# Another order for the products, sums and parts of a Winograd-type matmul kernel

## The chip, the cores and the metric

The kernel runs on one core of one Trainium2 chip. The time is that of one execution on the device in microseconds, the median of several runs. The core's engines are named as in the profile: PE (matmuls), DVE, ACT and POOL (elementwise work), SP (issues nearly all DMAs). Each engine works off its own instructions in the order in which the program issues them and waits on semaphores for the others.

## The reference

Windowed attention (8 batches, 8 heads, 576 positions, head size 64, window 64) makes x with 512 channels per position; an MLP over positions and an MLP over channels follow.

```python
def _moe_ref(x, w_tok1, w_tok2, w_ch1, w_ch2):
    xt = x.transpose(0, 2, 1)
    h = np.maximum(xt @ w_tok1, 0.0) @ w_tok2      # 576 -> 256 -> 576
    u = x + h.transpose(0, 2, 1)
    h2 = np.maximum(u @ w_ch1, 0.0) @ w_ch2        # 512 -> 1536 -> 512
    return (u + h2).astype(np.float32)
```

All values are float32. The change touches the second half, h2 and the sum with u, for 8 x 576 = 4608 positions.

## The kernel before

**Parts.** Every operand of a product is split into a high part (`hi`, a cast to fp32r on ACT) and a low part (`lo`, the source less the high part, a subtraction on DVE or POOL), and each product of two 128-wide operands is three matmuls: hi x hi, hi x lo, lo x hi. A matmul has 512 columns.

**First half** (to about 260 us of the span): attention and the MLP over positions. It stores u in DRAM by chunks of 512 positions (`u_dram`). Nine chunks, 0 to 8, are left for the MLP over channels.

**Plain chunks 0, 1, 2** (260 to 477 us). For each, `gemm1` makes 12 blocks of 128 hidden channels (slots `ft` 0 to 11, 12 matmuls each), followed by `relu_split`: ACT writes ghi, DVE glo. `gemm2` multiplies these with the second weights for four column blocks `ct`; `add_out` adds the result to u on DVE and stores it. Chunk 0 does all 12 slots and then the four blocks; chunks 1 and 2 do it in two halves of six slots (18 matmuls a block). `load_u` and `split_u` fetch and split the next chunk's u (four parts, `uhi` on ACT, `ulo` on DVE). Beside this run generators that the loops push on with `next`:

- `late_steps`: conversion of the second weights in chunk 0 (seven steps per block)
- `weight_steps` (`steps`): sums of the first weights for the pairs, in tiles of the pool `pw`, stored in `w1s`; 16 steps
- `weight_steps2` (`steps2`): the same for the second weights. Six sets, each of five steps: blocks of 512 KB are loaded from DRAM into `w2t`, summed on DVE, cast on ACT into `w2p` and subtracted on DVE; eight stores of 128 KB go to `w2s`. `w2t` and `w2p` lie where the first pair's operands of m7 and m5 are to lie (tags c4, c5), and `w2p` holds one set.
- `quarter_steps2` (`steps3`): stores of weights that are used without a sum, 12 of 384 KB, in chunk 2.

In chunk 2 the first pair's operands are made as well: `load_raw` loads four blocks of u, `sums` and `sum4` form sums on DVE, `prep` splits an operand into `comb`.

**Pairs** (3,4), (5,6), (7,8), 477 to 888 us. Two chunks at a time, the product with each weight matrix uses seven block products instead of eight, `PRODUCTS` = m1, m6, m7, m5, m2, m4, m3. `INTO` gives the PSUM bank of each: m1 and m2 share bank 0, m7 and m4 bank 2, m5 and m3 bank 3, and the later product of the two adds to the bank after the earlier one has been read. A pair has three groups (`grp`), each of two slots `pair_f` (f even with `fi` 0, f odd with `fi` 1; 42 matmuls each) and an output stage `pair_op` (84 matmuls). `pair_f` combines the products on ACT and DVE in x1, x2, x3, applies the ReLU (`block`: r22, r11, r21, r12) and splits. `combine` forms the sums t1, t2, r12, t1 and their parts; for the even slot it is pushed on during the odd one, for the odd slot it runs in the output stage. In the output stage, for t = 0 and 1, the products are added to `common` (m1, m6) or to `ufs` (all others) on DVE; in the last group of a pair `common` is added to `ufs` as well and the result is stored. There (`more`, unless the pair is the last) the next pair's operands are made too: `prep(q + 1, m, 0)` for half of them in the odd slot and the start of the stage, `prep(q + 1, m, 1)` during t = 1. All loads and stores are issued from SP, in program order.

## Time and profile before

| | us |
|---|---|
| median of 3 runs | 891.22 (889.02 to 892.72) |
| the profiled execution | 892.58 |
| its span | 890.6 |
| mean granted clock | 0.971 |
| PE busy | 830.0 (93%) |
| DVE busy | 630.7 (71%) |
| ACT busy | 422.7 (47%) |
| POOL busy | 191.1 (21%) |

A row of groups reads: line, engine, operation, what it writes <- what it reads, shapes, count | busy time, mean ns | idle time of the engine just before and what ended it. A row of waits reads: who waited <- for whom, total us, times, longest us. A row of the timeline: start, duration, instruction, and in brackets the idle time before it with what ended it. A row of windows: the stretch, its length, busy time and count of PE, weight loads, DVE, ACT and POOL, granted clock, share of the DMA engines, GB/s. PE's rows overlap, since matmuls are pipelined.

### The profile page before, as it was taken

The numbers are of one execution on the slowest core, as the hardware profiler recorded it, in microseconds if no ns is written. First come the engines' busy times: TensorE is split into PE (matmuls) and PEld (weight loads), VectorE is DVE, ScalarE is ACT, GpSimd is POOL, SyncE is SP. The second block draws the span as 40 slices with busy tenths as digits, with TensorE's granted clock in tenths as the row PEclk, the third lists the DMA queues.
The fourth block names the chain that finished last, engine by engine and source line by source line (L and its number), as shares of the span: only waits on it lengthen the run. The fifth ranks groups of instructions, "written<-read, shape, count | busy, mean of one in ns | idle before, by whom it ended". The sixth has DMA issues, their size and how long they took to land.

```text
span 890.6 us, 15820 instructions
## 1 busy us (share of the span) xinstructions
PE 830.0 (93%) x5752; PEld 666.2 (75%) x5752; DVE 630.7 (71%) x1545; ACT 422.7 (47%) x1173; POOL 191.1 (21%) x181
## 2 busy tenths in 40 slices
PE   8989999999999899989899999968999986999997
PEld 6668888888898688857688686746777764777775
DVE  5978888898828946774454858676667678675767
ACT  6978988898834303232132423342515152424251
POOL 3623444343310000000001111125202023311021
PEclk9999999999999999989899999997999989999999
DMA  9837877875456477669919482626945444845412
GB/s 351 274 105 253 268 233 242 280 266 196 141 176 214 124 240 209 203 204 290 334 42 381 180 294 100 232 90 220 338 176 204 166 166 151 323 175 194 168 53 94
DMA packets 91357, 185.90 MB, mean 209 GB/s; under 512 B 8848, under 2 KB 56336, under 8 KB 89360
## 3 DMA queue, kind: packets, MB, share of 16 engines
q1 hardware_dynamic: 89168, 183.07, 60.1%
q10 hardware_dynamic: 2112, 1.84, 0.6%
q8 instruction: 45, 0.74, 0.3%
q14 instruction: 32, 0.26, 0.1%
HBM read 140.84 MB, written 44.04 MB: 208 GB/s over the span
## 4 chain that ended last, share of the span: by engine, by line
PE 21%; DVE 16%; ACT 13%; issue 4%; DMA 4%; SPq 1%; ACTq 0%; DVEq 0%
PE op L1041 11%; PE gp L1005 5%; ACT w2hi_r L991 5%; ACT ghic L955 4%; DVE w2lo_r L964 3%; DVE w1lo L959 3%; PE op L665 3%; ACT w1hi L955 2%; PE gp L656 2%; DMA out<-uf 2%; DVE x L1015 1%; DVE w2lo_r L977 1%; DVE m L129 1%; DMA w2t<-w_dram 1%; DVE w2lo_r L967 1%
## 5 line engine op out<-in xcount | busy, mean ns | idle before, releaser
L1005 PE MATMUL gp<-m,w1hi 128*128 128x512 f32 x504 | 158.3, 396 | 7.8 <-DVE x L1013 5.3
L1005 PEld LDWEIGHTS gp<-m,w1hi 128*128 128x128 f32 x504 | 94.4, 190 | 32.6 <-DVE x L1013 9.2
L329 ACT ACTIVATE e<-e,nm 128x128 f32<-128x128 f32 x288 | 112.2, 397 | 5.9 <-DVE nm L321 5.8
L959 POOL TENSOR_TENSOR gloc<-w2hi_r,ghic 128x512 fp32r<-128x512 f32 x18 | 23.2, 1292 | 411.7 <-ACT ghic L955 404.3
L1005 PE MATMUL gp<-m,w1lo 128*128 128x512 f32 x252 | 98.9, 392 | 0.0
L1045 DVE TENSOR_TENSOR uf<-op,uf 128x512 f32<-128x512 f32 (+1 forms) x91 | 61.6, 683 | 28.4 <-PE op L1041 26.3
L1041 PE MATMUL op<-ghic,w2hi 128*128 128x512 f32 (+1 forms) x145 | 60.2, 415 | 15.4 <-DVE uf L1045 7.9
L321 DVE CUSTOM_DVE_ANT_0 e<-s,mask 128x128 f32<-128x128 f32 x288 | 65.3, 285 | 12.1 <-PE s L306 12.0
L991 ACT ACTIVATE w2hi_r<-x 128x512 f32<-128x512 f32 x54 | 34.1, 631 | 65.2 <-DVE x L1015 47.1
L1041 PE MATMUL op<-gloc,w2hi 128*128 128x512 f32 (+1 forms) x145 | 58.7, 405 | 0.0
L1041 PE MATMUL op<-ghic,w2lo 128*128 128x512 f32 (+1 forms) x145 | 58.7, 405 | 0.0
L665 PE MATMUL op<-ghi,w2hi 128*128 128x512 f32 x128 | 53.0, 414 | 5.3 <-ACT ghi L643 5.3
L656 PE MATMUL gp<-uhi,w1hi 128*128 128x512 f32 x144 | 56.1, 390 | 0.1
L656 PE MATMUL gp<-ulo,w1hi 128*128 128x512 f32 x144 | 56.0, 389 | 0.0
L656 PE MATMUL gp<-uhi,w1lo 128*128 128x512 f32 x144 | 56.0, 389 | 0.0
L329 ACT ACTIVATION_READ_ACCUMULATOR e<-e,nm 128x1 f32 x288 | 56.0, 194 | 0.0
L1005 PEld LDWEIGHTS gp<-m,w1lo 128*128 128x128 f32 x252 | 47.8, 190 | 10.3
L665 PE MATMUL op<-glo,w2hi 128*128 128x512 f32 x128 | 53.1, 414 | 2.5 <-DVE glo L644 2.5
L665 PE MATMUL op<-ghi,w2lo 128*128 128x512 f32 x128 | 52.1, 407 | 0.0
L1041 PE MATMUL op<-w1lo,w2hi 128*128 128x512 f32 (+1 forms) x91 | 38.8, 426 | 14.0 <-DVE w1lo L959 14.0
L129 POOL TENSOR_TENSOR xlo<-x,xhi 128x512 fp32r<-128x512 f32 x32 | 41.6, 1300 | 45.3 <-ACT xhi L126 44.6
L1009 ACT COPY x<-gp 128x512 f32<-128x512 f32 x18 | 10.5, 583 | 84.1 <-PE gp L1005 84.1
(166 smaller groups left out, 2029.3 us busy)
## 6 DMA issues: line engine op xcount, KB each, us to landing
v<-vh SPq DMA_DIRECT2D x36, 512.0 KB, 4.2
w1hi<-w1s SPq DMA_DIRECT2D x18, 896.0 KB, 4.8
w1lo<-w1s SPq DMA_DIRECT2D x18, 896.0 KB, 6.5
w2hi<-w2s SPq DMA_DIRECT2D x18, 896.0 KB, 4.7
w2lo<-w2s SPq DMA_DIRECT2D x18, 896.0 KB, 6.5
raw<-wc SPq DMA_DIRECT2D x32, 384.0 KB, 4.7
q<-qh SPq DMA_DIRECT2D x36, 256.0 KB, 4.5
k<-kh SPq DMA_DIRECT2D x7, 1280.0 KB, 8.2
```

The lines of the kernel that those rows point to most:

```text
L129: eng_lo.tensor_sub(lo, src, hi.bitcast(F32))
L321: nc.vector.tensor_tensor_reduce(out=e[:, h], in0=s[:, h], in1=mk, scale=-scale, scalar=MAX_F32, op0=ALU.add, op1=ALU.min, accum_out=nm[:, ...
L329: nc.scalar.activation(e[:, h], e[:, h], AF.Exp, bias=nm[:, g:g + 1], scale=-1.0, accum_out=sm[:, g:g + 1])
L656: nc.tensor.matmul(gp, w[:, w1_at(ft, ct)], x[:, ct], start=(k == 0), stop=(k == 3 * NCT - 1))
L665: nc.tensor.matmul(op, w[:, at], x[:, cols], start=(first and k == 0), stop=(last and k == 3 * len(gs) - 1), skip_group_check=not (first a ...
L955: nc.scalar.copy(ops_g[fi][m][0], made[MADE[m]])
L959: eng.tensor_sub(lo, made[MADE[m]], hi.bitcast(F32))
L964: sub(r["t1"], r["r12"], r["r11"])
L991: nc.scalar.activation(made[name], src, AF.Relu)
L1005: nc.tensor.matmul(b, w[:, at], c[:, h, t], start=(n < 4 and k == 0), stop=(k == 5), skip_group_check=True)
L1041: nc.tensor.matmul(bank[t][INTO[m]][:, cols], w[:, at], ops_g[fi][m][h][:, cols], start=(n < 4 and fi == 0 and j == 0), stop=(j == 2), ski ...
L1045: eng.tensor_add(ufs[c][:, ct, cols], x, ufs[c][:, ct, cols])
```

## The change

No matmul and no operand is added or left out; the order in the queues of PE, ACT, DVE, POOL and SP changes.

- Chunk 0: the split of chunk 1's u goes from slot 8 to the four column blocks. Chunk 1: the split of chunk 2's u goes from slot 8 to slots 10 and 11.
- `steps` go from one to two per column block in the first half of chunk 1. `steps2` go from chunk 1 alone (from the first half's blocks on) to slots 10 and 11 and the second half's blocks of chunk 1 (18 steps) and the first half of chunk 2 (two per slot, the rest at the first block).
- The first pair's operands for t = 0 (m1, m6, m7, m5, m2) go from slots 1 and 2 of chunk 2 to the column blocks after slot 5, those for t = 1 two slots later.
- `prep` can make the high or the low part alone. `combine` makes m5's low part earlier.
- `pair_f`: m1's low part waits in `later` until m4's addition is issued; m2's low part of the odd slot is made in the output stage on DVE instead of POOL. At a pair's first slot (from the second pair on) the t = 0 halves of m1, m6, m7, m5 come first.
- `pair_op`: m1's products with the odd slot come after m6's with the even one; both m2 products come before the t loop instead of between m5 and m4. Next-pair parts have other places and engines; in all but the last pair `common` is added on POOL at the end of the stage.

```diff
@@ -700,9 +700,8 @@
                 split_w2()
             if ft == 3:
                 ul[1] = load_u(1, pu)
-            if ft == 8:
-                split_u(ul[1])
         for ct in range(NCT):
+            split_u(ul[1], (ct,))
             for _ in range(7):
                 next(late, None)
             assert all(n in finished for n in range(len(jobs) - 16, len(jobs) - 12 + 4 * ct))
@@ -858,12 +857,15 @@
 
         SOURCE = {"m1": "r11", "m6": "t2", "m7": "r12", "m5": "t1", "m2": "r21", "m4": "r11", "m3": "r22"}
 
-        def prep(q, m, t, eng=None):
+        def prep(q, m, t, eng=None, part=None):
             if (q, m) not in comb:
                 pool = pb if HOME[m] == "c6" else pu
                 comb[q, m] = pool.tile([P, 2, 2, CHUNK], F32R, name=f"{m}_{q}", tag=HOME[m], bufs=1)
-            c = comb[q, m]
-            split(nc.scalar, eng or nc.vector, c[:, 0, t], c[:, 1, t], raws[SOURCE[m]])
+            c, x = comb[q, m], raws[SOURCE[m]]
+            if part != "lo":
+                nc.scalar.copy(c[:, 0, t], x)
+            if part != "hi":
+                (eng or nc.vector).tensor_sub(c[:, 1, t], x, c[:, 0, t].bitcast(F32))
 
 
         steps, steps2, steps3 = weight_steps(), weight_steps2(), quarter_steps2()
@@ -880,31 +882,23 @@
                     gemm1(j, ft, u, g[-1])
...
-                        if half == 1 and ft % 2:
+                        if ft == 3:
+                            ul[j + 1] = load_u(j + 1, pu)
+                        if ft >= NFT - 2:
+                            split_u(ul[j + 1], (2 * (ft - NFT) + 4, 2 * (ft - NFT) + 5))
                             next(steps2, None)
-                    if last and half == 0:
+                    elif half == 0:
                         next(steps3, None)
...
+                        for _ in range(2):
+                            next(steps2, None)
+                    else:
                         if ft == 6:
                             load_w1(0)
+                        if ft == 8:
                             sums()
-                        if ft in (7, 8):
-                            for m in (("m1", "m6"), ("m7", "m5", "m2"))[ft - 7]:
-                                prep(0, m, 1)
-                        if ft == 9:
+                        for m in {8: ("m1", "m6"), 9: ("m7", "m5"), 10: ("m2",)}.get(ft, ()):
+                            prep(0, m, 1)
+                        if ft == 11:
                             sum4()
...
+                    if j == 1 and half == 0:
+                        for _ in range(1 if ct == NCT - 1 else 2):
+                            next(steps, None)
+                    elif j == 1:
+                        for _ in range(4):
                             next(steps2, None)
...
+                    elif half == 0:
+                        if ct == 0:
+                            for _ in steps2:
+                                pass
+                            sums()
+                        for m in (("m1", "m6"), ("m2",), ("m7",), ("m5",))[ct]:
                             prep(0, m, 0)
+                        if ct == NCT - 1:
+                            load_raw(0, 1)
+                    else:
+                        if ct in (0, 1):
+                            load_w2s(ct)
+                        if ct == 1:
+                            sums(False)
+                            sum4()
+                            for m in ("m4", "m3"):
+                                prep(0, m, 0)
...
             parts_hi(fi, "m6")
+            parts_lo(fi, "m5", nc.vector)
             yield
...
-            parts_lo(fi, "m5", nc.vector)
-            yield
...
             parts_lo(fi, "m7", nc.vector)
             yield
+            yield
             parts_lo(fi, "m4", nc.vector)
-            x1 = x1s[fi]
+            x1, later = x1s[fi], []
...
-                    parts_lo(fi, m, eng)
-
+                    if eng is nc.vector:
+                        later.append(m)
+                    elif eng is not None:
+                        parts_lo(fi, m, eng)
+
+            def product(m, ts, first):
+                n, b, c = PRODUCTS.index(m), bank[INTO[m]], comb[q, m]
+                for k, t in enumerate(ts):
+                    at = slice(o + (n * 2 + t) * P, o + (n * 2 + t + 1) * P)
+                    for j, (w, h) in enumerate(((w1hi, 0), (w1hi, 1), (w1lo, 0))):
+                        nc.tensor.matmul(b, w[:, at], c[:, h, t], start=(first and n < 4 and k == j == 0),
+                                         stop=(k == len(ts) - 1 and j == 2), skip_group_check=True)
...
+            more = q + 1 < len(pairs)
+            begin = q > 0 and f == 0
             next(rest, None)
+            if begin:
+
+                for m in PRODUCTS[:4]:
+                    product(m, (0,), True)
...
+                b = bank[INTO[m]]
+                if begin and n < 4:
+                    product(m, (1,), False)
+                else:
+
+                    product(m, (1, 0) if q == 0 and m in ("m4", "m3") else (0, 1), True)
...
-                    block("r21", x2, "m2", nc.gpsimd)
+                    while later:
+                        parts_lo(fi, later.pop(), nc.vector)
+
+                    block("r21", x2, "m2", None if fi else nc.gpsimd)
...
-                if q + 1 < len(pairs):
-                    if f == NH - 2 and m == "m1":
-                        sums()
-                    if f == NH - 1 and n < 4:
-                        prep(q + 1, m, 0, nc.gpsimd if n % 2 else nc.vector)
+                if more and f == NH - 2 and m == "m1":
+                    sums()
+                if more and f == NH - 1 and n < 5:
+                    prep(q + 1, m, 0, part="hi")
+                    if n < 2:
+                        prep(q + 1, m, 0, nc.gpsimd, part="lo")
...
-            def product(t, m, fi, cols=slice(0, CHUNK)):
+            def product(t, m, fis=(0, 1), first=False, cols=slice(0, CHUNK)):
...
+                for fi in fis:
+                    at = slice(t * SLOT + (n * 2 + fi) * P, t * SLOT + (n * 2 + fi + 1) * P)
+                    for j, (w, h) in enumerate(((w2hf, 0), (w2hf, 1), (w2lf, 0))):
+                        nc.tensor.matmul(bank[t][INTO[m]][:, cols], w[:, at], ops_g[fi][m][h][:, cols],
+                                         start=(n < 4 and fi == j == 0), stop=(fi == fis[-1] and j == 2),
+                                         skip_group_check=True)
...
+            WHERE = {"m7": (1, 2), "m5": (1, 2), "m4": (0, 2), "m3": (1, 0)}
+
+            def evict(t, m):
+                b = bank[t][INTO[m]]
+                if m == "m1" and grp == 0:
+                    nc.scalar.copy(common[t], b)
+                elif m in ("m1", "m6"):
+                    nc.vector.tensor_add(common[t], b, common[t])
+                elif m == "m2":
+                    add(0, t, b)
+                    if last:
+                        store(0, t)
+                else:
+                    c, ct = WHERE[m]
+                    add(c, ct + t, b)
+
+            def add_common(t, m, eng):
+                c, ct = WHERE[m]
+                add(c, ct + t, common[t], eng)
+                store(c, ct + t)
+
...
             for t in range(2):
-                for fi in range(2):
-                    product(t, "m1", fi)
-            for m in PRODUCTS[1:4]:
+                product(t, "m1", (0,))
+            for t in range(2):
+                product(t, "m6", (0,))
+            for t in range(2):
+                product(t, "m1", (1,))
+            for m in ("m7", "m5"):
                 for t in range(2):
-                    product(t, m, 0)
-            for _ in combine(1):
+                    product(t, m, (0,))
+            ops = combine(1)
+            if more:
+
+                prep(q + 1, "m7", 0, part="lo")
+                prep(q + 1, "m5", 0, part="lo")
+                prep(q + 1, "m2", 0, nc.gpsimd, part="lo")
+            for n in range(3):
+                next(ops)
+            parts_lo(1, "m2", nc.vector)
+            evict(0, "m1")
+            product(0, "m2")
+            next(ops)
+            evict(1, "m1")
+            if not (final and last):
+                product(1, "m2")
+            next(ops)
+            if more:
+                sum4()
+                prep(q + 1, "m4", 0, part="hi")
+                prep(q + 1, "m3", 0, part="hi")
+                prep(q + 1, "m3", 0, nc.gpsimd, part="lo")
+            next(ops)
+            evict(0, "m2")
+            if not (final and last):
+                evict(1, "m2")
+            for _ in ops:
                 pass
             if more:
-                for m in PRODUCTS[4:]:
-                    if m == "m4":
-                        sum4()
-                    prep(q + 1, m, 0, nc.gpsimd if m == "m4" else nc.vector)
+                prep(q + 1, "m4", 0, part="lo")
                 load_raw(q + 1, 1)
...
             for t in range(2):
                 end = final and last and t == 1
...
+                for m in ("m6", "m7", "m5", "m4", "m3"):
+                    product(t, m, (1,) if m in PRODUCTS[:4] else (0, 1))
+                    evict(t, m)
+                    if end and m in ("m5", "m4", "m3"):
+                        add_common(t, m, nc.vector)
+                    if more and t == 0 and m == "m3":
                         sums()
-                    if more and t == 1:
-                        if m == "m4":
-                            sum4()
-                        prep(q + 1, m, 1, nc.gpsimd if m in ("m7", "m2", "m3") else nc.vector)
+                        for x in PRODUCTS[:4]:
+                            prep(q + 1, x, 1, part="hi")
+                        prep(q + 1, "m1", 1, nc.gpsimd, part="lo")
+                    if more and t == 1 and m == "m6":
+                        prep(q + 1, "m6", 1, part="lo")
+                        prep(q + 1, "m7", 1, nc.gpsimd, part="lo")
+                        prep(q + 1, "m2", 1, part="hi")
+                        prep(q + 1, "m3", 1, part="hi")
+                    if more and t == 1 and m == "m7":
+                        prep(q + 1, "m5", 1, part="lo")
+                        sum4()
+                        prep(q + 1, "m4", 1, part="hi")
+                    if more and t == 1 and m == "m4":
+                        prep(q + 1, "m2", 1, nc.gpsimd, part="lo")
+                        prep(q + 1, "m4", 1, part="lo")
+                if end:
+
+                    for part in range(LAST_PARTS):
+                        cols = slice(part * CHUNK // LAST_PARTS, (part + 1) * CHUNK // LAST_PARTS)
+                        product(t, "m2", cols=cols)
+                        add(0, t, bank[t][0][:, cols], cols=cols)
+                        store(0, t, cols)
+                elif last and final:
+                    for m in ("m5", "m4", "m3"):
+                        add_common(t, m, nc.gpsimd)
                 load_w2s((q * NGRP + grp + 1) * 2 + t)
+            if more:
+                prep(q + 1, "m3", 1, part="lo")
+                for t in range(2):
+                    for m in ("m5", "m4", "m3"):
+                        add_common(t, m, nc.gpsimd)
```

65 lines of the change are left out of this document (removed).

## The prediction

> **What bounds the kernel now.** Read first: the page, for how full TensorE is and when its clock drops.
>
> ```profile
> span 890.6 us, 15820 instructions
> ...
> PE   830.0 (93%) x5752; PEld 666.2 (75%) x5752; DVE 630.7 (71%) x1545; ACT 422.7 (47%) x1173; POOL 191.1 (21%) x181
> ...
> PEclk9999999999999999989899999997999989999999
> ```
>
> TensorE (PE) is the bound; the profiled execution took 892.6 us, 2.0 around its span, 1.4 over the median of 891.2. The change leaves the matmuls as they are, so only PE's pauses can move. Second, the stages by windows, beside the pace in the chain of waits: 24 matmuls in 5.45 us, 0.227 each.
>
> ```profile
> 518.70 5.45 PE gp L1005 x24
> ...
> 260.10:292.60 32.50, 32.50 (x145) 26.95 (x144) 21.78 (x46) 11.76 (x25) 0.00 (x0) 1.00 0.58 182
> 292.60:330.60 38.00, 34.98 (x145) 27.96 (x144) 25.89 (x57) 9.72 (x21) 0.00 (x0) 0.96 0.63 189
> 330.60:394.80 64.20, 59.89 (x249) 47.91 (x248) 46.55 (x94) 21.12 (x43) 0.00 (x0) 0.95 0.68 202
> ...
> 411.10:434.70 23.60, 20.07 (x73) 14.63 (x72) 12.63 (x24) 7.36 (x15) 0.00 (x0) 0.86 0.94 308
> ...
> 518.60:560.40 41.80, 40.00 (x170) 30.98 (x169) 29.00 (x42) 14.24 (x24) 5.30 (x4) 1.00 0.57 201
> 560.40:619.20 58.80, 45.80 (x170) 34.68 (x169) 41.56 (x58) 21.85 (x38) 19.16 (x14) 0.89 0.49 170
> ...
> 702.80:759.50 56.70, 45.84 (x170) 34.68 (x169) 42.01 (x57) 20.93 (x37) 18.25 (x14) 0.88 0.50 173
> ...
> 843.00:890.60 47.60, 40.63 (x175) 31.11 (x173) 31.87 (x47) 14.23 (x24) 9.17 (x7) 0.99 0.23 83
> ```
>
> After the window come its length, then PE's busy time and rows, and the granted clock third from the end. The first row is undisturbed: 145 rows in 32.5 us. Losses: chunk 0's second product 5.5 us (38.0 less 32.5); chunk 1 7.7 (64.2 less 249 x 0.227); chunk 2 7.0 (23.6 less 73 x 0.227). The other windows are cut at one point of successive groups of a pair, 168 matmuls or 38.1 us each (rows over an edge count twice): an inner group loses 3.6 (six such), the two groups that end a pair 20.7 and 18.6, the last some 6 beside its tail. That is 87 us.
>
> Third, who ends PE's waits:
>
> ```profile
> PE op L1041 <- DVE w1lo L959: 14.0, 26, 1.0
> PE op L1041 <- DVE uf L1045: 7.9, 4, 3.0
> PE op L1041 <- DVE w2lo_r L1077: 7.5, 2, 3.7
> PE gp L1005 <- DVE x L1013: 5.3, 8, 1.9
> PE op L665 <- ACT ghi L643: 5.3, 3, 3.0
> PE op L665 <- DVE glox L644: 3.0, 2, 2.5
> ```
>
> Nearly all are queues on DVE and ACT: a low part, or an addition that frees a bank, stands behind other work. The waits are less than the losses, since a long one also halves the clock:
>
> ```profile
> 575.40:578.70 3.30, 1.48 (x7) 0.87 (x5) 2.48 (x5) 1.34 (x4) 0.00 (x0) 1.00 0.17 68
> 578.80:582.10 3.30, 1.87 (x7) 1.26 (x8) 2.77 (x4) 1.21 (x3) 1.28 (x1) 1.00 0.00 0
> 595.90:599.20 3.30, 0.72 (x4) 0.24 (x2) 2.04 (x3) 1.14 (x2) 1.26 (x1) 1.00 0.00 0
> 599.30:606.00 6.70, 5.65 (x13) 4.46 (x14) 3.79 (x7) 0.62 (x1) 1.28 (x1) 0.50 0.69 229
> ...
> 718.80:722.10 3.30, 1.41 (x6) 0.86 (x5) 2.85 (x5) 1.62 (x3) 0.40 (x1) 1.00 0.00 0
> 722.20:728.90 6.70, 5.72 (x14) 3.55 (x12) 4.23 (x5) 2.88 (x5) 3.30 (x3) 0.50 0.22 38
> ```
>
> Stretches of 3.3 us with 4 or 6 matmul rows are followed by clock 0.50; the one with 7, which holds a wait of 1.9 (the longest on L1013), is not. So with some 2.1 us of one such stretch idle the next 3.4 us run at half speed, which costs 1.7.
>
> **The change, part by part.** Durations for the walks below:
>
> ```profile
> 498.20 0.68 DVE L977 TENSOR_TENSOR w2lo_r<-w2hi_r,w2lo_r 128x512 f32<-128x512 f32 x1
> 498.80 0.68 DVE L1020 TENSOR_TENSOR x<-gp,x 128x512 f32<-128x512 f32 x1
> ...
> 500.24 0.62 ACT L955 CAST w1hi<-w2hi_r 128x512 fp32r<-128x512 f32 x1
> 500.76 0.63 ACT L991 ACTIVATE w2hi_r<-x 128x512 f32<-128x512 f32 x1
> ...
> 500.94 1.49 POOL L959 TENSOR_TENSOR w1lo<-w2hi_r,w1hi 128x512 fp32r<-128x512 f32 x1 [3.21 <-ACT w1hi L955]
> ...
> 501.43 1.55 DVE L964 TENSOR_TENSOR w2lo_r<-w2hi_r 128x512 f32<-128x512 f32 x1
> ...
> 507.07 0.50 PE L1041 MATMUL op<-w1lo,w2hi 128*128 128x512 f32 x1 [0.97 <-DVE w1lo L959]
> ...
> 881.44 0.50 PE L1041 MATMUL op<-ghic,w2hi 128*128 128x512 f32 x1 [0.74 <-DVE uf L1045]
> ```
>
> DVE starts an operation every 0.60 us and its result stands after 0.68; ACT every 0.52, 0.62. A DVE operation with both inputs in SBUF that meets a running POOL operation ends about 0.5 after it (501.43 lasted 1.55, POOL running to 502.43).
>
> Chunk 0 (gain 3.9). The four splits for chunk 1, on ACT and DVE, leave the queue ahead of the relu splits:
>
> ```profile
> 294.07 2.49 DVE L129 TENSOR_TENSOR ulo<-uf,uhi 128x512 fp32r<-128x512 f32 x4
> ...
> 303.55 0.68 DVE L644 SCALAR_TENSOR_TENSOR glox<-gp,ghix 128x512 fp32r<-128x512 f32 x1
> ```
>
> The last glox then ends 2.4 earlier, at 301.8. PE wants it as the 35th matmul of the product that starts at 292.6, at 300.3, so with the refill after a wait (0.11, by which the second matmul after one is late) 1.6 of 5.5 remains, and no clock loss. The splits return at 0.6 each in product two, where DVE ends its conversions long before PE asks (bound 0 to 1).
>
> Chunk 1 (gain 7.7, bounds 5 to 7.7). The splits, 2.5 us of DVE in one piece now, go two by two to slots 10 and 11, and the second weights' sums leave the slots but for these two; the first weights' sums go two to a column block, 3.3 of DVE's 4.1 us there. The first of the second sums waits on DVE for a load of 512 KB, with slot 11's relu split behind it. That load is issued once SP has issued the last store of the first sums, in slot 8, lands about when DVE reaches the sum, and slot 11's parts stand 1.4 before PE wants them. If it came 3 later, 1.6 and some clock would be lost.
>
> Chunk 2 (loss 3.5; bounds: 7 gained, 8 lost). Before, sums() waits on DVE for the raw blocks and PE waits 3.0 on ghi; this sums() moves to the half's products and that wait goes. But 13 of 31 steps of the second weights' sums now run here, beside the quarters' stores.
>
> ```profile
> 422.56 0.69 DVE L851 TENSOR_TENSOR t<-r,r 128x512 f32<-128x512 f32 x1 [6.36 <-DMA r<-u_dram]
> ...
> 400.52 0.41 ACT L775 CAST w2p<-w2t 128x256 fp32r<-128x256 f32 x1 [0.27 <-DMA w2s<-w2p]
> ...
> GB/s 381 377 395 381 324 312 293 154 107 134 137 239 331 365 384 382 383 377 378 378 325 192 159 277 335 374 383 383 383 383 386 384 387 439 423 430 405 380 93 0
> ...
> w2s<-w2hi SPq DMA_DIRECT2D x5, 384.0 KB, 5.6
> ...
> w2s<-w2p SPq DMA_DIRECT2D x10, 128.0 KB, 2.6
> ```
>
> Each cast into w2p waits until the store of that part from the step set before has landed, and stands in ACT's queue ahead of the next ghi. At some 384 GB/s a 384 KB store takes 1.0 us, a 128 KB one 0.35. With T the start of chunk 2, SP's queue is: four raw loads (landed T+11.4), then per slot two quarter stores (2.0 together) between sets of four part stores (1.4) and a last load (1.4). So m5's part of the fourth set lands at T+13.8, of the fifth T+22, its m6 T+25.5. Behind the casts that wait for them ghi comes at T+18 (slot 3), 22.4 (slot 4), 26 (slot 5), while PE wants them at T+18.4, 20 and 20.7 at its own pace: waits of 0.9, 3.7 and 2.9, and some 3 of half clock: 10.5 against 7.0 now. The lower bound takes casts that never wait, the upper DMA at three quarters of that rate. The first pair's operands are made in the products after that: m5's tile is that of w2p, free when the last store lands (T+34), and is asked for at T+40; SP's raw loads and load_w1 behind them land 20 us and more before the pairs begin.
>
> Inner groups (gain 2.2 each, 13.2 for six). Times from the odd slot's start; its 42 matmuls end at +9.5. m1's low part now follows m4's addition, so x2, x3, r22 and r12 come some 0.5 earlier and the wait on L1013 goes (0.4 a group). ACT has r12 at +12.2. Then DVE starts: t1 12.25, t2 12.97, low m5 13.62, r12 14.22, low m2 14.82, m1's addition 15.42 to 16.11, low m6 16.02, m1 for t=1 16.62, t1 again 17.22, low m7 17.82, m2 18.42, m2 for t=1 19.26 (when PE has it), low m4 19.87, m6 20.47, m7 21.07 to 21.76. POOL is idle, so none is stretched. PE: m1's second half comes 12 matmuls later than before and no longer waits for its low part; 30 matmuls bring it to 16.34, where m2 wants bank 0, free at 16.11: a thin 0.2. Two m2 products end at 19.06, nine matmuls on at 21.10 m4 wants m7's addition to have left its bank. Before, m2 stood between; now m4 waits to 21.81, 0.8 with the refill (such a wait is the row at 881.44), and for t=1, where DVE is free, 0.4. So 1.2 remains, and 0.2 in steps too small to list, of 3.6 (bounds 0.8 to 2: DVE with a free moment at t=0, or one more operation of 0.6 ahead).
>
> The two groups that end a pair (gain 14.3). Of the next pair's low parts 7 stand on POOL and 7 on DVE instead of 6 and 8, while m2's own goes from POOL to DVE; they leave the odd slot, but for two on POOL. Walk again: ACT has three casts more, so r11 leaves its bank at +10.6 and m1 for t=1 waits 0.5. DVE: low m4 stretched by POOL to 13.75, two low parts, then combine from 14.87 and m1's addition 18.04 to 18.73; PE wants it at 16.9: 2.0. Behind sum4, two m2 additions and the two low m4 (one stretched by POOL to 25.35) m7's addition ends at 26.6; PE wants it at 23.65: 3.1. For t=1 three sums (the first stretched by POOL to 31.6) and low m6 stand ahead: m7 ends at 34.8 for 31.5: 3.4; low m5 and sum4 then hold m5's: 1.0. That is 10.1 with the refills. A wait w puts 2.1 idle into one stretch of 3.4 in (1.3 + w - 2.1) / 3.4 of its positions, 0.65 and 0.75 for the two long ones: 1.4 x 1.7 = 2.4. So 12.5 is left of 20.7 and 18.6 (bounds 6, POOL losing each tie, to 19). The six additions of POOL now come last and end some 6 us into the next slot; behind them on SP stand their stores, the uf loads (two of 1 MB) and load_w1, which land near +17 of the next pair, where uf is added to near +27. load_w2s stands ahead of them. The half-products at the next pair's start give its operands time and cost nothing.
>
> The last group: 1.2 of the inner kind, 0.5 more because only one m2 product stands early, and 1.4 before the second half of m2 as now: 3.1 of 6.0, gain 2.8.
>
> The clock once more. The trace halves it after a stretch with 6 of 15 matmuls. The Trainium skill ("TensorE: Matmul & The Clock Gate", Why this matters for your kernels) says to avoid idle gaps over some 3 us, one idle window bringing half speed. The trace differs: 722.2 to 728.9 was halved after a wait of 1.9. By the page only the wait of 3.4 would count, once per pair end, and the sum would be 1.4 lower.
>
> **Sum.** 3.9 + 7.7 - 3.5 + 13.2 + 14.3 + 2.8 = 38.4 off 892.6: 854.2, or 852.8 at the median. I take 853.
>
> **The rivals.**
> (a) The stores land sooner or the casts don't hold ACT, and chunk 2 loses nothing: 842. For it: casts waited only 0.3 each before. Against: then no quarter stores stood between.
> (b) Pair ends stay as they are, DVE being held by POOL: 853 + 14 = 867. For it: POOL's parts now stand where combine runs on DVE. Against: DVE's two low parts leave the odd slot, where the wait of 1.9 began.
> (c) The change does not do what it says: low parts are only late at other products, and only chunks 0 and 1 gain, 6 or less: 885 to 891. Against it, the 12-matmul cover.
> (d) Slower: m2's early product waits in all nine groups, since its low part is now DVE's and m1's addition follows it. It decides from 3.1 us each: over 2.1 half clock adds 1.7, and 9 x 4.8 eats 38.4 and 4.5 (0.5%). At 3.5 it gives 853 + 47 = 900. The walk has 0 inside and 2.0 at pair ends.
>
> **How the numbers follow.** Forecast 0.60 (own range 845 to 862), (a) 0.16, (b) 0.15, (c) 0.05, (d) 0.04. 838 to 872 takes in (a), (b) and the bounds of chunk 2, and leaves out (c), (d) and both ends together, under 2 in 10. About 0.5% (4.5 us) is what a measurement can tell from no change: faster 0.92, same 0.04, slower 0.04.
>
> **What would show it.** Right: glox waits of about 1.5 us, none in chunk 1; in chunk 2 ACT's w2p casts waiting for w2s stores, PE for ghi; inner groups of 39.3 us whose waits are on uf (L1045's successor) and not on w1lo; pair ends of about 50.6 us. Wrong: chunk 2 without waits (too high), inner groups at 41 or pair ends with two half-clock stretches each (too low).

## The result and the profile after

The changed kernel takes 852.4 us (median; 850.8 to 854.1), the kernel before on the same chip 890.1 (888.5 to 892.7): a ratio of 0.957, with a 95% interval of 0.954 to 0.961. The prediction was 853. The profiled execution took 850.8 us. The page of the changed kernel, the lines that answer to the first ones shown of before:

```profile
span 849.0 us, 15802 instructions
...
PE 806.2 (95%) x5752; PEld 658.8 (78%) x5752; DVE 627.1 (74%) x1552; ACT 423.0 (50%) x1173; POOL 182.9 (22%) x174
...
PEclk9999999999999999999799999998999999899999
```

PE's count of matmuls is that of before, and DVE, ACT and POOL are busy as long as before to within 8.2 us: what changed is the time between operations. PE's own busy time fell by 24 us, since the trace counts a matmul at half clock with 0.63 us and one behind a wait with 0.50, the others with 0.39. The windows of the changed kernel, cut where each stage begins (chunk 0's product, chunk 1, chunk 2's first product, an inner group, a pair end, the next group, the second pair end, the last group):

```profile
289.90:323.50 33.60, 32.94 (x145) 26.95 (x144) 25.13 (x54) 9.03 (x20) 0.00 (x0) 1.00 0.65 196
323.50:388.80 65.30, 65.30 (x290) 54.06 (x289) 47.08 (x92) 20.64 (x42) 0.00 (x0) 1.00 0.71 211
405.10:433.80 28.70, 21.09 (x74) 14.68 (x73) 14.17 (x28) 8.03 (x17) 0.00 (x0) 0.82 0.83 271
505.80:545.20 39.40, 38.75 (x170) 31.33 (x169) 28.25 (x43) 14.27 (x24) 3.88 (x3) 1.00 0.60 215
545.20:594.80 49.60, 41.08 (x169) 32.02 (x168) 41.55 (x57) 21.84 (x38) 17.78 (x13) 0.95 0.52 186
594.80:635.10 40.30, 39.65 (x170) 32.04 (x169) 28.57 (x42) 15.15 (x26) 8.73 (x7) 0.98 0.71 266
674.40:724.20 49.80, 40.90 (x169) 32.08 (x169) 41.63 (x57) 21.84 (x38) 17.77 (x13) 0.95 0.52 187
804.20:849.00 44.80, 39.29 (x175) 31.52 (x173) 31.04 (x48) 14.27 (x24) 7.76 (x6) 1.00 0.26 96
```

Chunk 1 is now without a gap: 65.3 us of PE busy in 65.3, at full clock. An inner group takes 39.4 for 38.1 of matmuls. Chunk 2's first product takes 28.7 for 16.3 of matmuls, and the pair ends 49.7, both with a granted clock below 1. Who ends PE's waits, in the changed kernel:

```profile
PE op L1065 <- DVE uf L1070: 18.8, 14, 2.9
PE op L665 <- ACT ghi L643: 7.1, 4, 2.6
PE op L1065 <- DVE w2lo_r L1082: 3.4, 2, 1.7
...
PE op L665 <- DVE glox L644: 0.7, 1, 0.7
```

The 14.0 us on w1lo and the 5.3 on x are gone. The largest line is now the additions into uf, 14 waits: one of 0.5 in each of the six inner groups (a second, of 0.1, is too short for the list), three in each of the two pair ends, two in the last group. Where the text below says by how much a matmul is late, it means the time beyond the pace of 0.227 us, which is 0.15 or more above the idle time that the views show.

The table gives the time from the first matmul of a stage to the first of the next (of the last group, to its last matmul's end), read from the matmul rows of each kernel's trace. Without any wait the columns would be 32.6, 65.3, 16.3, and 38.1 for each group; the last group has a tail besides. The other kernels are those of the experiments below.

| kernel | chunk 0 product | chunk 1 | chunk 2 product 1 | group 1 | group 2 | pair end | group after | pair end 2 | group after | last |
|---|---|---|---|---|---|---|---|---|---|---|
| before | 38.1 | 73.6 | 23.3 | 41.3 | 41.8 | 58.7 | 41.8 | 56.7 | 41.7 | 44.4 |
| after | 33.6 | 65.3 | 28.7 | 39.3 | 39.4 | 49.7 | 40.3 | 49.8 | 40.5 | 41.6 |
| pairs_only | 35.8 | 72.7 | 22.9 | 39.3 | 39.4 | 49.8 | 39.4 | 49.5 | 40.3 | 41.5 |
| plain_only | 33.5 | 65.3 | 28.8 | 41.3 | 41.8 | 56.5 | 41.9 | 56.6 | 41.7 | 44.4 |
| later_only | 38.9 | 73.3 | 23.0 | 39.1 | 39.5 | 52.4 | 39.2 | 50.9 | 39.2 | 42.2 |
| m1_now | 33.6 | 66.1 | 30.3 | 43.9 | 44.1 | 51.7 | 42.8 | 52.0 | 42.8 | 45.0 |
| m2_back | 33.4 | 65.3 | 28.7 | 38.4 | 39.6 | 48.0 | 38.4 | 48.0 | 38.4 | 41.7 |
| m7_first | 33.4 | 65.3 | 29.0 | 38.3 | 38.4 | 49.7 | 38.4 | 49.7 | 40.0 | 40.6 |
| quarters_late | 33.8 | 65.3 | 24.3 | 39.4 | 39.4 | 48.4 | 39.4 | 49.6 | 40.1 | 41.6 |
| pace_only | 33.7 | 65.3 | 24.0 | 39.4 | 39.4 | 51.0 | 40.1 | 49.5 | 40.5 | 41.6 |
| paced | 33.8 | 65.3 | 16.3 | 39.4 | 39.4 | 48.3 | 39.7 | 49.6 | 40.1 | 41.6 |
| ends | 33.8 | 65.3 | 28.5 | 38.3 | 38.3 | 41.4 | 44.8 | 41.3 | 44.2 | 40.6 |
| best | 33.9 | 65.3 | 16.3 | 38.3 | 38.4 | 41.3 | 44.4 | 41.3 | 44.4 | 40.6 |
| best_dve | 33.7 | 65.3 | 16.3 | 38.3 | 38.4 | 41.3 | 43.2 | 41.3 | 43.2 | 40.6 |

Ratios below are to the kernel before, run on the same chip beside each kernel; 0.01 is 8.9 us.

### The profile page after: what moved, and what is told of

The parts are those of the page before. It is cut to its first block, busy times and chain, and to the rows that moved or that the text cites. A ratio compares the mean times of both kernels' runs of the same rounds, so it can differ in the third digit from the quotient of the medians.

```text
span 849.0 us, 15802 instructions
## 1 busy us (share of the span) xinstructions
PE 806.2 (95%) x5752; PEld 658.8 (78%) x5752; DVE 627.1 (74%) x1552; ACT 423.0 (50%) x1173; POOL 182.9 (22%) x174
## 4 chain that ended last, share of the span: by engine, by line
PE 67%; DVE 16%; ACT 7%; DMA 5%; issue 3%; SPq 1%; POOL 0%; ACTq 0%; DVEq 0%
PE gp L1010 17%; PE op L1065 13%; PE op L665 10%; PE gp L656 6%; PE h L396 5%; PE up L444 5%; PE xp L348 4%; DVE uf L1070 3%; PE s L306 3%; ACT e L329 3%; PE pp L336 2%; PE up L437 2%; DVE w2lo_r L1082 2%; DMA w_dram<-w 1%; DVE gloc L965 1%
## 5 line engine op out<-in xcount | busy, mean ns | idle before, releaser
L1010 PE MATMUL gp<-m,w1hi 128*128 128x512 f32 x504 | 156.7, 393 | 0.0
L965 POOL TENSOR_TENSOR gloc<-w2hi_r,ghic 128x512 fp32r<-128x512 f32 x18 | 23.3, 1294 | 414.5 <-ACT ghic L961 405.9
L1010 PEld LDWEIGHTS gp<-m,w1hi 128*128 128x128 f32 x504 | 95.8, 190 | 20.2
L1010 PE MATMUL gp<-m,w1lo 128*128 128x512 f32 x252 | 98.6, 391 | 0.0
L321 DVE CUSTOM_DVE_ANT_0 e<-s,mask 128x128 f32<-128x128 f32 x288 | 65.3, 285 | 10.7 <-PE s L306 10.5
L1028 ACT COPY x<-gp 128x512 f32<-128x512 f32 x18 | 10.5, 584 | 100.7 <-PE gp L1010 100.7
L1065 PEld LDWEIGHTS op<-ghic,w2hi 128*128 128x128 f32 x145 | 27.4, 189 | 39.8 <-DVE uf L1070 28.5
L665 PE MATMUL op<-ghi,w2hi 128*128 128x512 f32 x128 | 51.3, 401 | 7.1 <-ACT ghi L643 7.1
L1010 PEld LDWEIGHTS gp<-m,w1lo 128*128 128x128 f32 x252 | 47.8, 190 | 10.1
L665 PE MATMUL op<-glo,w2hi 128*128 128x512 f32 x128 | 51.3, 401 | 0.5 <-DVE glo L644 0.5
L129 POOL TENSOR_TENSOR xlo<-x,xhi 128x512 fp32r<-128x512 f32 x32 | 41.6, 1299 | 43.7 <-ACT xhi L126 43.0
```

Source lines behind the costliest of these rows:

```text
L129: eng_lo.tensor_sub(lo, src, hi.bitcast(F32))
L321: nc.vector.tensor_tensor_reduce(out=e[:, h], in0=s[:, h], in1=mk, scale=-scale, scalar=MAX_F32, op0=ALU.add, op1=ALU.min, accum_out=nm[:, ...
L665: nc.tensor.matmul(op, w[:, at], x[:, cols], start=(first and k == 0), stop=(last and k == 3 * len(gs) - 1), skip_group_check=not (first a ...
L1010: nc.tensor.matmul(b, w[:, at], c[:, h, t], start=(first and n < 4 and k == j == 0), stop=(k == len(ts) - 1 and j == 2), skip_group_check= ...
L1065: nc.tensor.matmul(bank[t][INTO[m]][:, cols], w[:, at], ops_g[fi][m][h][:, cols], start=(n < 4 and fi == j == 0), stop=(fi == fis[-1] and ...
```

## The experiments

**Do the two halves of the change add up?** pairs_only has the new pairs and the old plain chunks, plain_only the reverse.

> The pair part of the change alone (low parts by parts, m2's products ahead, additions of POOL last); chunks 0 to 2 as before. Theory (the parts are independent, the pairs give 13.2 + 14.3 + 2.8 of the predicted sum): 30.3 less than before, about 860 us; in the trace no wait on w1lo, chunk 2 with the single wait of some 3 us on ghi that the kernel before has. Rival (pairs and chunks depend on each other, e.g. the pairs' first operands come late without the new chunk 2): a wait on the first pair's operands and over 863. Rival (the changed kernel's gain came mostly from the chunks): 875 or more.

> The plain-chunk part of the change alone (splits and second weights' sums moved); pairs as before. Theory: chunk 0 gains 3.9 to 4.5, chunk 1 7.7 to 8.3, chunk 2 loses 3.5 to 5: about 7 to 8 less than before, 882 to 883 us, and the six inner groups still at 41.8. If the parts are independent, the gains of this and of the pairs alone add up to the changed kernel's 38. Rival (a pair part depends on the new chunks): the two gains differ from 38 by more than 3.

Measured: 0.965 (0.962 to 0.968) and 0.991 (0.989 to 0.993). Multiplied, 0.956, beside 0.957 for both: as far as intervals of 0.003 can tell, the parts are independent. The pairs carry 31 us, the chunks 8, in which chunk 2's loss is already counted. In the table most stages of each half stand as in the kernel that they come from. Chunk 0's product is an exception: with the same old code it takes 35.8, 38.1 and 38.9 in pairs_only, before and later_only, at a mean granted clock of 1.00, 0.96 and 0.91.

**Which piece of the pairs carries it?** Three kernels: the changed one without `later`, the changed one with m2 back in its place, and the kernel before with `later` alone.

```diff
# m1_now (on the changed kernel, undone)
-                    if eng is nc.vector:
-                        later.append(m)
-                    elif eng is not None:
+                    if eng is not None:
                         parts_lo(fi, m, eng)
# m2_back (on the changed kernel): product and evict of m2 out of the stage's start, and
                 for m in ("m6", "m7", "m5", "m4", "m3"):
                     ...
+                    if m == "m5" and not end:
+                        product(t, "m2")
+                        evict(t, "m2")
# later_only (on the kernel before): those lines of `later` put in, and behind m4's addition
+                    while later:
+                        parts_lo(fi, later.pop(), nc.vector)
```

> The changed kernel with one piece undone: m1's low part stands on DVE right behind its block again, not behind m4's addition. Theory (the predicted 0.4 a group: x2, x3, r22 and r12 come one DVE operation later, and PE waits for a bank of gp): waits on x return in the even or odd slots, 0.4 to 0.6 in each of nine groups, 4 to 5 us more than the changed kernel, about 857. Rival (PE has enough products between, the wait on x was gone by the other moves): 852, no wait on x.

> The changed kernel with m2's products and additions of the pairs' second product back behind m5's for each t; the new order of the rest stays. Theory (the twelve matmuls of m2 cover the low parts of the odd slot): the waits on w1lo return, for m6's low part some 0.4 and for m7's and m1's addition up to 2 per group, less the 1.2 of m4's waits that go since m2 stands between again: 1 to 2 a group more, 861 to 870. Rival (m4's waits are the only thing that the place of m2 changes): 1.2 a group less, 842 to 845.

> The kernel before with one piece of the change alone: m1's low part stands behind m4's addition on DVE in every slot of the pairs; all else as before. Theory (undoing this piece cost the changed kernel 33 us: DVE idles 2.0 to 2.5 us in front of that low part, with m4's addition, r12 and all of the next sums behind it, so this piece alone carries most of the pairs' gain): the inner groups come down from 41.8 to some 39.5, each pair end and the last group by 3 or more, 890 - 25 = 862 to 870. Rival (the piece is only worth something together with the new order of m2, m6 and the low parts, which leave no other operation as late): 884 to 890, waits on w1lo as before.

m1_now: 0.994 (0.992 to 0.997). This one piece undone costs 33 us, not the 4 to 5 expected; between the profiled executions it is 33.4, of which 29.5 lie in the nine groups of the pairs. DVE in the odd slot, first of m1_now (its group starts at 514.22), then of the changed kernel (505.77):

```profile
532.09 0.69 DVE L982 TENSOR_TENSOR w2lo_r<-w2hi_r,w2lo_r 128x512 f32<-128x512 f32 x1
535.26 0.69 DVE L965 TENSOR_TENSOR w1lo<-w2hi_r,w1hi 128x512 fp32r<-128x512 f32 x1 [2.48 <-ACT w1hi L961]
535.87 0.69 DVE L965 TENSOR_TENSOR gloc<-w2hi_r,ghic 128x512 fp32r<-128x512 f32 x1
536.47 0.68 DVE L1037 TENSOR_TENSOR x<-gp,x 128x512 f32<-128x512 f32 x1
```

```profile
523.02 0.69 DVE L965 TENSOR_TENSOR gloc<-w2hi_r,ghic 128x512 fp32r<-128x512 f32 x1
523.65 0.69 DVE L1039 TENSOR_TENSOR x<-gp,x 128x512 f32<-128x512 f32 x1
525.59 0.69 DVE L965 TENSOR_TENSOR w1lo<-w2hi_r,w1hi 128x512 fp32r<-128x512 f32 x1 [1.25 <-ACT w1hi L961]
```

m1's low part (w1lo) waits for its cast on ACT, which stands there behind four other operations. At its old place that wait is 2.48 long, and m4's addition (L1037, x<-gp,x) stands behind it, 22.3 after the group's start; with `later` it runs at 17.9. The wait that is left, 1.25, stands ahead of m3's addition (L1045), and ACT waits only 0.17 for that one, as the second of the rows below shows. Behind m4's addition come r21, r12 and the whole of `combine`. ACT's ReLU of r12, of m1_now and of the changed kernel:

```profile
538.44 0.63 ACT L997 ACTIVATE w2hi_r<-x 128x512 f32<-128x512 f32 x1
```

```profile
526.92 0.63 ACT L997 ACTIVATE w2hi_r<-x 128x512 f32<-128x512 f32 x1 [0.17 <-DVE x L1045]
```

That is 24.2 against 21.2 after the group's start: the chain that feeds the output stage starts 3.1 us earlier. The kernel before has the same stall, with its w1lo at 20.5 and r12 at 23.7 (its group starts at 518.53):

```profile
539.00 0.78 DVE L959 TENSOR_TENSOR w1lo<-w2hi_r,w1hi 128x512 fp32r<-128x512 f32 x1 [1.96 <-ACT w1hi L955]
```

later_only confirms it from the other side: 0.972 (0.970 to 0.975), 25 of the pairs' 31 us from moving one subtraction in each slot. Its inner groups take 39.1 to 39.5, as those of the whole change. The nine groups together (two of them are not in the table) take 410.1 us before, 381.5 in later_only and 379.3 in the changed kernel.

m2_back: 0.950 (0.946 to 0.954), 7 us less than the changed kernel. The theory (m2's 12 matmuls as a needed cover) falls. The waits on w1lo do come back, but small, here the longest of the inner groups and the two of the first pair end:

```profile
532.66 0.50 PE L1065 MATMUL op<-w1lo,w2hi 128*128 128x512 f32 x1 [0.84 <-DVE w1lo L965]
...
573.03 0.50 PE L1065 MATMUL op<-w1lo,w2hi 128*128 128x512 f32 x1 [1.89 <-DVE w1lo L965]
575.44 0.52 PE L1065 MATMUL op<-w1lo,w2hi 128*128 128x512 f32 x1 [1.44 <-DVE w1lo L965]
```

In the table a pair's first group loses 0.3 in this kernel (there m1 is copied by ACT, so DVE has two additions fewer), the second 1.5, against 1.2 to 1.3 for both in the changed kernel, and a pair end with the group behind it 10.2 instead of 13.8 to 14.1. The early m2 does not help: where it removes waits on w1lo, it exposes m4, which then asks for m7's bank. The other pieces of the pairs (m6's early products, the places of the next pair's operands) were not taken apart; m2_back has them all, and its nine groups take 371.7 us, 9.9 less than those of later_only.

**Is m4's wait one operation long?** m7_first changes the order in the t loop to m7, m6, m5, m4, m3.

> The changed kernel with m7's second half-product and its addition ahead of m6's for each t of the pairs' second product. Theory (m4 waits 0.7 at t=0 and 0.3 at t=1 because m7's addition is one DVE operation of 0.6 us too late): the inner groups lose 0.2 instead of 1.2, 7 us for seven groups; at the pair ends t=0's wait of 3.0 shrinks by 0.6 and t=1's goes ahead of the low parts that stood before it, 1 to 3 each: 840 to 844. Rival (DVE is as full with either order, and m7's own low part, the last of combine, is now asked for three matmuls earlier): a new wait on glo of m7 takes the place, 850 to 854.

0.950 (0.948 to 0.953). Inner groups lose 0.2 to 0.3 instead of 1.2, as expected. The pair ends themselves gain nothing (49.7): m7's wait at t = 1 shrinks, and m5's addition, now behind the operands that stood behind m7's, is waited for instead, 3.1 us late at 593.19 against 1.8 in the changed kernel. Of m5's successor, in PE's timeline of m7_first:

```profile
593.19 0.79 PE L1065 MATMUL op<-ghic,w2hi 128*128 128x512 f32 x1 [2.70 <-DVE uf L1070]
```

So at the pair ends this order of the additions only hands the wait on; what DVE does between them stays.

**Where should the next pair's operands stand?** ends (with m7 first) moves them as its expectation says.

> The kernel with m7 first, and the next pair's operands moved in the groups that end a pair: the low parts of m7, m5 and m4, sum4 and the load of the second raw blocks each behind one of t=0's additions, the sums of t=1 behind m5's addition of t=1, the rest behind the last. Theory (each wait there is an addition behind those operations on DVE; DVE has room between t=0's and t=1's additions): of some 12 us per pair end 2 to 4 are left and no stretch at half clock, 843.6 - 17 = 825 to 829. Rival (DVE is full over the whole group, so that the operations come too late for the next pair instead): waits on m in the first products of the next pair take the place, 836 to 844, or more if the raw blocks land late.

0.942 (0.939 to 0.945). Half theory, half rival. The pair ends come down from 49.7 to 41.4, but the group behind goes up to 44.8, from 40.3 in the changed kernel and 38.4 in m7_first, on which this one is built. The waits that took the place, in PE's timeline of this kernel:

```profile
591.72 0.73 PE L1010 MATMUL gp<-m,w1hi 128*128 128x512 f32 x2 [1.95 <-ACT x L1028]
595.34 1.22 PE L1010 MATMUL gp<-m,w1hi 128*128 128x512 f32 x2 [1.40 <-DVE x L1032]
```

The first is m2 (L1010, of the next pair's first slot) asking for m1's bank, whose copy stands on ACT behind a cast that waits 2.1 for sum4 (r, L856) on DVE:

```profile
590.56 0.62 ACT L866 CAST m<-r 128x512 fp32r<-128x512 f32 x1 [2.09 <-DVE r L856]
591.09 0.58 ACT L1028 COPY x<-gp 128x512 f32<-128x512 f32 x1
```

Of the 13.8 to 14.1 us that a pair end and the group behind it lose in the changed kernel (11.9 and 13.5 in m7_first), 9.3 to 10.0 are still lost, only elsewhere.

**What holds chunk 2?** ACT there, in the changed kernel:

```profile
406.23 0.41 ACT L774 CAST w2p<-w2t 128x256 fp32r<-128x256 f32 x1 [7.10 <-DMA w2s<-w2p]
...
407.16 0.59 ACT L643 ACTIVATE ghi<-gp 128x512 fp32r<-128x512 f32 x1
...
414.36 0.40 ACT L774 CAST w2p<-w2t 128x256 fp32r<-128x256 f32 x1 [3.22 <-DMA w2s<-w2p]
414.67 0.59 ACT L643 ACTIVATE ghi<-gp 128x512 fp32r<-128x512 f32 x1
```

Casts into w2p wait 7.1 and 3.2 us for stores of the step set before to land, with the next ghi behind. Three kernels take the queue apart.

```diff
# quarters_late: chunk 2's quarter stores from the first half's slots to the second half's
                     elif half == 0:
-                        next(steps3, None)
                         for _ in range(2):
                             next(steps2, None)
                     else:
+                        next(steps3, None)
# pace_only: chunk 1's blocks push steps2 less, raw loads in slot 4 and not ahead of the chunk
-                        for _ in range(4):
+                        for _ in range(3):
                             next(steps2, None)
...
-                load_raw(0, 0)
+                        if ft == 4:
+                            load_raw(0, 0)
# paced: both
```

> The changed kernel with chunk 2's quarter stores (384 KB each, two a slot) moved from the first half's slots to the second half's. Theory (each w2p cast on ACT waits for its store, and these land late because the quarter stores stand between them on SP): the four waits on ghi (1.3, 2.1, 2.8, 1.9 us) and the half-clock stretch of chunk 2 go, some 12 us less than the changed kernel, about 840. Rival (the casts and additions themselves are too much for ACT and DVE in these slots, or the loads of the sums' inputs come late): waits on ghi stay, 850 to 853. Rival (the stores only move the trouble: load_w1 or load_raw behind them in the second half come late): waits appear in the second half's products or in the first pair, 845 to 860.

> The kernel with the quarter stores in the second half, and besides the second weights' steps three to a column block instead of four in chunk 1's products (five are left for chunk 2's products) and the raw blocks' loads behind slot 3. Theory (a set of five steps takes some 6 us, cast, low part, stores landed, next cast; at one set in 5.4 us in chunk 1's products ACT falls 5 us behind, and this is what still makes ghi late in slots 3 to 5): the waits of 1.4, 1.1 and 1.2 and the half clock go, 7 us less than with late quarter stores alone, about 836. Rival (casts and sums in the slots are one chain between ACT and DVE that is too long at two steps a slot, whatever stands before): waits of about 1 stay, 842 to 845.

> The changed kernel with the second weights' steps three to a column block in chunk 1's products and the raw blocks' loads behind slot 3; the quarter stores stay in the first half's slots, between the sets' stores. Theory (chunk 2's waits have two causes that add up: ACT is 5 us behind when the chunk starts, and the quarter stores and loads stand between a set's stores; late quarter stores alone gave 4.4 us, both together 12.4): some 5 to 8 us less than the changed kernel, 844 to 847, with waits of about 1 us left on ghi. Rival (the pace alone is the cause, the quarter stores fit beside it): 840, no waits on ghi. Rival (the quarter stores alone hold ACT as long as they stand there, as the predicted queue of SP had it): 850 to 853.

0.950 (0.949 to 0.952), 0.945 (0.941 to 0.948) and 0.953 (0.949 to 0.958). Chunk 2's first product takes 24.3, 16.3 and 24.0 for 28.7 in the changed kernel: late stores alone give 4.4, the slower pace alone 4.7, the two together all 12.4, without a wait left:

```profile
404.70:421.10 16.40, 16.40 (x75) 13.56 (x74) 11.62 (x25) 5.65 (x12) 0.00 (x0) 1.00 0.74 236
```

(75 rows in 16.4 us, clock 1.00, of paced.) The theory of quarters_late, that the stores between are the one cause (840), did not hold: 843.5, with three waits on ghi left. pace_only came out within its 844 to 847, with two waits on ghi (1.2 and 2.5); it moves the raw loads as well as the steps, and which of the two helps was not separated. The expectation of paced was right for the place and 4 short for the time: its median of 840 is 12 less than the changed kernel's 852. With late quarter stores alone a cast still waits 4.6 us for a store, and behind the next two ghi casts wait for sums instead (1.1 and 1.5 us), which stand behind glo on DVE. That the lag so hands itself on between ACT and DVE is a reading of these rows, not tested; paced has waits of 1.1 there too, and PE waits for none of them.

```profile
404.17 0.41 ACT L774 CAST w2p<-w2t 128x256 fp32r<-128x256 f32 x1 [4.60 <-DMA w2s<-w2p]
...
407.36 0.41 ACT L774 CAST w2p<-w2t 128x256 fp32r<-128x256 f32 x1 [1.13 <-DVE w2t L792]
...
410.40 0.40 ACT L774 CAST w2p<-w2t 128x256 fp32r<-128x256 f32 x1 [1.47 <-DVE w2t L785]
```

**The pieces together.** best is paced with the order of ends, and with sum4 and the last operands behind the next pair's first additions. best_dve has in addition the six additions that end a pair on DVE.

```diff
# best, in pair_f behind each product of a pair's first slot
+                if begin:
+                    if m == "m1":
+                        sum4()
+                        prep(q, "m4", 1, part="hi")
+                    elif m == "m7":
+                        prep(q, "m4", 1, part="lo")
+                    elif m == "m5":
+                        prep(q, "m3", 1, part="lo")
+                    elif m == "m3":
+                        ... # the last pair's six add_common, on POOL
# best_dve: two of the six behind each of m2, m4, m3, on nc.vector
```

> Late quarter stores with the slower pace of the second weights' steps, m7 first and the moved operands at the pair ends together; and, against the waits of some 2 us each on x that the first products of the next pair showed, sum4 and m4's and m3's parts of t=1 behind the next pair's first additions (m1's copy, m7's, m5's), and POOL's six additions behind its first m3. Theory (the pieces add up: 852 - 12 for chunk 2 - 7 for the inner groups and the last - 6 to 9 for each pair end): 815 to 823, with chunk 2 at 32.6 a half and the pair ends at 40 to 42. Rival (DVE has no room for the next pair's operands wherever they stand): 9 to 10 us stay lost per pair end as with the moved operands alone, about 826. Rival (uf and w1 behind the late additions' stores come too late): a wait on uf or w1 in the first groups of a pair, 830 or more.

> The fastest kernel so far with the six additions that end a pair on DVE instead of POOL, two behind each of m2, m4 and m3 in the next pair's first slot. Theory (POOL's six additions of 1.7 us each stretch every DVE operation with both inputs in SBUF from 0.7 to 1.2 to 1.8 over 10 us of the next slot, and the wait of 2.9 on x and its half clock stand there): 3.6 us of DVE in a slot where it idles some 3, the wait of 2.9 and the half clock go, 824 - 2 x 4 = 815 to 818. Rival (DVE has no 3.6 us free there): the waits move to the next slot or to the first products behind it, 822 to 826.

best: 824.2 us, 0.928 (0.927 to 0.930), faster than the kernel before and the changed one, by 28 us against the latter in the medians and 26 by the ratios. It misses its theory's 815 to 823. Chunk 2 and the inner groups are free; a pair end with the group behind it loses 9.5 (41.3 + 44.4 less 76.2), as in the first rival. best_dve: 0.928 (0.925 to 0.931), the same in time, as in its rival; its group after a pair end is 1.2 shorter, but the wait of 2.9 on x was replaced by one of 2.2 on ACT's copy of m1, and its profiled execution lost 3.0 before chunk 0. So what is left at the pair ends is not settled by a move from POOL to DVE. That DVE's amount of work, not its order, is the limit there fits these kernels: the windows of best at the end of this document show DVE busy 3.41 us of 3.41 around the waits, in part since POOL stretches its operations, and in best_dve, with POOL idle, it is busy 3.37 of 3.40 us at the wait (590.00 to 593.40). It was not tested by taking work away, and over the whole group behind a pair end DVE is busy 38.5 of 44.4 us in best, so a better order is not ruled out.

## Why the prediction was right, point by point

By the first matmuls of the stages; an entry is the gain, with the group behind counted to a pair end where the half clock runs over.

| step | predicted | measured |
|---|---|---|
| chunk 0 | 3.9 | 4.5 |
| chunk 1 | 7.7 | 8.3 |
| chunk 2 | -3.5 | -5.0 |
| six inner groups | 13.2 | 14.0 |
| two pair ends | 14.3 | 13.9 |
| last group | 2.8 | 2.9 |
| up to chunk 0 (unchanged code) | 0 | 2.9 |
| sum | 38.4 | 41.6 |

Without the part before chunk 0, 38.7 stand beside the predicted 38.4; the medians differ by 37.7. That the sum fits so much better than its terms is luck: chunk 2 is 1.5 worse than reckoned, the other terms together 1.7 better.

- Chunk 0: a wait of 0.7 on glox and 0.9 lost, for 1.6 predicted. Against pairs_only, where the same old code met no half clock, the gain is 2.2. Chunk 1: nothing lost, as predicted. The gain is 8.3 and not 7.7 because the prediction's window of chunk 1 ends at 394.8, while chunk 2 begins at 404.55: 0.6 was lost behind the window. The window of chunk 2's product is as early; from 421.23 to 444.57, where that product lies, the loss is 7.0 as well.
- Chunk 2: the wait was the right one, casts that hold ghi until stores have landed, but the reckoning left out a cause, and 12.4 were lost for 10.5. There are four waits on ghi (1.3, 2.1, 2.8 and 1.9 late) instead of three of 0.9, 3.7 and 2.9: ghi of slots 2 to 5 comes 18.4, 21.8, 25.9 and 29.3 after the chunk's start, where 18, 22.4 and 26 were reckoned for slots 3 to 5, one slot later. The reckoning gave ACT no arrears at the chunk's start. The changed kernel's trace shows them: chunk 1's blocks push a set of five steps each 5.1 us (four per 18 matmuls), and the ghi of chunk 2's first slot is written at 396.5, 5.0 us after that slot's last matmul. In pace_only that ghi comes 4.7 earlier, at 3.0 instead of 7.7 after the chunk's start, and 7.7 of the 12.4 stay lost. So the queue of stores by itself seems to cost less than the 10.5 reckoned for it, and the arrears left out make up for that; the raw loads, moved in pace_only, keep this from being exact.
- Inner groups: 1.2 left, of it 0.8 at t = 0 and 0.4 at t = 1 as walked. But the reason given for the gain was wrong in its weights. That m1's low part follows m4's addition was put at 0.5 us, and the end of the waits on w1lo was laid to the 12 matmuls ahead of m1's second half (which comes 9 matmuls later than before, not 12). later_only and m1_now show the first at 2.6 to 3.1 us of head start and four fifths of the pairs' gain; later_only leaves m1's second half where it was, and its inner groups are as short as the changed kernel's. The walk came out because it was made from the new order's own operations, where both are contained; the comparison with before was the part that failed.
- Pair ends: losses of 0.5, 1.8, 2.5, 3.0 and 1.8 stand for the predicted 0.5, 2.0, 3.1, 3.4 and 1.0, and two stretches of 3.4 at half clock each; with the group behind, 12.5 and 12.9 for the 12.5 predicted. The waits come to 9.6 and 9.7 for 10.1, the half clock to some 3 for 2.4: two small errors that cancel. The sums ahead of m7 at t = 1 were a little cheaper, m5's addition waited longer.
- Rival (d), the early m2 held by m1's addition, came true at the pair ends alone (1.7 us of wait on w2lo_r, twice) and not inside. Rivals (b) and (c) did not occur. (a), a chunk 2 without loss, is what paced made by other means.
- The 2.9 before chunk 0 are no part of the change. Among the 14 profiled kernels chunk 0 starts at 256.9 to 258.6 or at 259.9 to 260.2, and the late ones (before, m7_first, best_dve) have the same code there as the early ones. In these three the first 60 us run at a mean granted clock of 0.94, in the changed kernel at 1.00.

## What to carry to other kernels

Look on each in-order engine for an instruction that waits for another engine while work that does not need it stands behind: the profile shows it as an idle time ended by that engine (2.0 us in front of w1lo here), and its price is what the whole chain behind it loses, not its own length. When a generator's steps are spread by hand, pace them by the slowest round trip (cast, low part, stores landed, next cast), and keep unrelated large transfers from between its stores. When a wait shrinks, ask at once who was second: m7's bank, then m5's, then the next pair's copy of m1 each took over.
